# Postmix of a talking-heads attention: one 64x112 product per block of keys instead of two of 64x56

## The chip, the cores and the metric

The kernel runs on one core of one Trainium2 chip. The metric is the device time of one execution in microseconds (us). Engines: PE is TensorE (PEld are its weight loads), DVE is VectorE, ACT is ScalarE, POOL is GpSimd, SP is the engine that issues most of the DMAs.

## The reference

All in fp32. Four batches, 12 heads, 448 positions, head size 64; the result of the attention goes through an elementwise mixture (`moe`) and a soft routing over 32 slots (`moe2`), which the change doesn't touch.

```python
scores = scale * np.matmul(q, k.transpose(0, 1, 3, 2))
scores = np.einsum('bhij,hg->bgij', scores, w_pre)      # premix
scores = scores - np.max(scores, axis=-1, keepdims=True)
attn = np.exp(scores)
attn = attn / (np.sum(attn, axis=-1, keepdims=True) + 1e-09)
attn = np.einsum('bhij,hg->bgij', attn, w_post)         # postmix
out = np.matmul(attn, v)
...
h = x @ w_in; g = h - np.tanh(h); x = g @ w_out         # moe
```

## The kernel before

The program has two halves. In the first, `talking_heads` computes the attention; in the second, `moe_and_slots` does the rest. The attention works in 16 chunks of up to 120 query positions of one batch, and in slots of up to 10 positions by 12 heads of a chunk. Slots are taken in pairs, 92 of them; a pair is s and s + 1 in the main loop, and each slot has two halves x of up to 5 positions, 60 rows of (head, position).

The path of a pair, in the order in which it is issued:

- `scores` (L279): q times k for a pair of heads, in fp32r, weights of 64 rows by up to 120 columns, copied by ACT (S, L287).
- `regroup` (L304): a DMA from SP brings the rows of one slot from S into a buffer D, so that heads lie on partitions. It is issued four slots ahead (`D_AHEAD`); there are six such buffers.
- `premix` (L313): w_pre times D into the PSUM tile pm, four products of 64 by 64 pieces, then the row maximum on DVE (mx, L317).
- `expo` (L325): the exponential on ACT into e, 64 rows of one slot above 64 rows of the other, 448 keys along the free axis. `guard`, `recip` and `norm` (L331, L335, L342) make wk, the postmix weights divided by the row sums.
- `postmix` (L356), four slots after the premix (`T_LAG`): for each half x, each of four blocks c of 112 keys and each slot i, e is the stationary operand and wk (60 columns) the moving one. The result has keys on partitions and goes into the PSUM tiles tm, one per slot. Before, a block of 112 keys is taken as two halves z of 56, which land on partitions 0 to 55 and 64 to 119.
- `gather` (L370, L373, L374): ACT copies tm into aT.
- `values` (L395): aT times v, contracted over the partitions that hold keys, accumulated over the four blocks, copied by DVE into xs (L405).

Key 4p + r of a head lies at column 112 r + p, so v must lie the same way over partitions: `load_v` (L170) brings it in two transfers, one for each half of the partitions. The eight partitions 56 to 63 and the eight from 120 on hold no key; they are zeroed once in v and tm by memsets.

The order on PE is the order of the code: in an even slot the premix of the new pair, then the postmix of the pair four slots back, then score products and other jobs (`k_pair` kx, `q_half` qx, `values` vx), which a small planner places by slot with fixed costs. Beside it runs the conversion of the weights of the second half on ACT, DVE and POOL (tiles f, fa), with its loads and stores on SP.

Of the kernel before, what the change touches and what calls it, by code (L numbers as in the profile page):

```python
# [17 lines left out]
NP = NH // 2  # L18
NR = 4
JP = SEQ // NR  # L20
JH = JP // 2
IH = 5
PASS = (512, 512, 512, 256)
LATE = 12
# [108 lines left out]
def talking_heads(tc, ident, q, k, v, w_pre, w_post, xd, box, follow):  # L133
    nc = tc.nc
# [20 lines left out]
    nat_k, nat_v, nat_q = {}, {}, {}  # L155
# [3 lines left out]
    attn_t = {}  # L159
# [6 lines left out]
    def load_v(b, hf):  # L166
        t = vns[(2 * b + hf) % 3]
        src = v[b, hf * NP:(hf + 1) * NP].rearrange("h (p r) d -> p h r d", r=NR)
        for z in range(2):
            nc.sync.dma_start(out=t[64 * z:64 * z + JH], in_=src[JH * z:JH * z + JH])  # L170
        nat_v[b, hf] = t

    def load_q(n):
# [44 lines left out]
    def small_bank(shape, name, tag=None):  # L218
        if tag is None:
            tag = min("xq", key=lambda z: ready[z][turn[z]]) if box["both"] else "x"  # L220
        i = turn[tag]
        turn[tag] = 1 - i
        ready[tag][i] = 10 ** 6
        pool = ps if tag == "x" else psq

        def read():
            ready[tag][i] = now[0]

        return pool.tile(shape, FP32, tag=tag, name=name, bufs=2), read
# [65 lines left out]
    def rows(s):  # L295
        n, kk = slots[s]
        o, m = chunks[n][3][kk]
        return n, o, m
# [48 lines left out]
    def postmix(s):  # L347
        es, wks = e_t.pop(s), wk_t.pop(s)
        xs = tms
        for x in range(2):  # L350
            for c in range(NR):
                for i in range(2):
                    for z in range(2):
                        h = slice(64 * i, 64 * i + 64)
                        j = JP * c + JH * z
                        nc.tensor.matmul(  # L356
                            xs[i][64 * z:64 * z + JH, x, c], lhsT=es[x][h, j:j + JH], rhs=wks[x][h],
                            start=True, stop=True)
        tm_t[s] = xs

    def gather(s):
        for i, x in enumerate(tm_t.pop(s)):
            n, o, m = rows(s + i)
            if o == 0:
                attn_t[n] = lt.tile([128, NR, NH, CHUNK], FP32, tag="aT", name="aT", bufs=2)
            c0 = sum(z for q, z in chunks[n][3] if q < o)
            out = attn_t[n].rearrange("p r h i -> p (r h) i")
            x = x.rearrange("p x r h i -> p (r h) x i")
            if m == 2 * IH:
                nc.scalar.activation(  # L370
                    out=out[:, :, c0:c0 + m].rearrange("p a (x i) -> p a x i", x=2), in_=x, func=ACTF.Copy)
            else:
                nc.scalar.activation(out=out[:, :, c0:c0 + IH], in_=x[:, :, 0], func=ACTF.Copy)  # L373
                nc.scalar.activation(out=out[:, :, c0 + IH:c0 + m], in_=x[:, :, 1, :m - IH], func=ACTF.Copy)  # L374
# [3 lines left out]
    def keep(n, dst, src):  # L378
        if n >= NC - 2:
            (nc.sync if n == NC - 2 else nc.scalar).dma_start(out=dst, in_=src)  # L380
        else:
            plan("load", now[0] + 1, lambda: nc.sync.dma_start(out=dst, in_=src))

    def values(n, g):
        b, i0, ni, _ = chunks[n]
        a = attn_t[n]
        if g == 0:
            xs_t[n] = lt.tile([128, NP, CHUNK], FP32, tag="xs", name="xs", bufs=1)
        xs = xs_t[n]
        x, read = small_bank([128, 2, CHUNK], "vx")  # L390
        for i in range(2):
            for c in range(NR):
                for e in range(2):
                    h = 4 * g + 2 * i + e
                    nc.tensor.matmul(  # L395
                        x[64 * e:64 * e + 64, i, :ni], lhsT=nat_v[b, h // NP][:, h % NP, c, :], rhs=a[:, c, h, :ni],
                        start=(c == 0), stop=(c == NR - 1))

        def rest():
            ms = [m for _, m in chunks[n][3]]  # L400
            w, top, c = len(ms), max(ms), 0
            natural = xs[:, 2 * g:2 * g + 2, :w * top].rearrange("p a (t w) -> p a w t", w=w)
            for m in sorted(set(ms), reverse=True):
                o, z = ms.index(m), ms.count(m)
                nc.vector.tensor_copy(  # L405
                    out=natural[:, :, o:o + z, :m],
                    in_=x[:, :, c:c + z * m].rearrange("p a (w t) -> p a w t", w=z))
                c += z * m
            read()
            if g == 2:  # L410
                t0, t1, p0 = b * SEQ + i0, b * SEQ + i0 + ni, 0
                for p, size in enumerate(PASS):
                    lo, hi = max(t0, p0), min(t1, p0 + size)
                    if lo < hi:
                        keep(n, xd[p][:, :, lo - p0:hi - p0], xs[:, :, lo - t0:hi - t0])
                    p0 += size

        return rest

    start = [sum(len(c[3]) for c in chunks[:n]) for n in range(NC + 1)]  # L420
# [11 lines left out]
    def calm(kind, lo, hi):  # L432
        return min(range(lo, hi + 1), key=lambda s: (load[kind][s], s))
# [20 lines left out]
    for m in range(1, NC):  # L454
        if chunks[m][1] + CHUNK >= SEQ and m + 1 < NC:
# [3 lines left out]
            for p in range(NP):  # L459
                t = w0 + HEAD_LAG + p // 2 * w // 3 + 1 + p % 2  # L460
# [9 lines left out]
    for m in range(NC):  # L470
        step = len(chunks[m + 1][3]) // 3 if m + 1 < NC - 1 else 2
        for g in range(3 if m + 1 < NC else 0):
            lo = start[m + 1] + T_LAG + 1 + g * step
            job(calm("pe", lo, lo + step - 1) if m + 2 < NC else lo, values, m, g, dve=0.41, pe=2.0)
    for b in range(NB):
        s0 = start[b * NC // NB]
        if b:
            fetch(s0 - 12, s0 + 8, 2.7, load_v, b, 0)
        fetch(s0 + (T_LAG + 10 if b else 8), s0 + 15, 2.7, load_v, b, 1)
# [18 lines left out]
    t = 2  # L498
    for i, j in enumerate(pieces):
        due = dues[i]  # L500
        t0 = max(t, due)
        a = calm("act", t0, t0 + 1)
        x = calm("dve", a + 1, a + 1 + (a <= due))
        load["dve"][x] += 0.54
        h = calm("dve", x, x + 1)
        load["dve"][h] += 0.47
        e = calm("dve", h, h + 1)
        load["dve"][e] += 0.74
        load["act"][a] += 0.41
        t = h  # L510
# [19 lines left out]
    vns = [lt.tile([128, NP, NR, HD], FP32, tag=f"vn{i}", name="vn", bufs=1) for i in range(3)]  # L530
# [1 line left out]
    wpost = kron("wpost", post_rows, 1.0, False)  # L532
    warm = ps.tile([128, 128], FP32, tag="p", name="warm")
    tms = [ps.tile([128, 2, NR, NH, IH], FP32, tag=f"t{i}", name="tm", bufs=1) for i in range(2)]
    for z in range(2):
        nc.vector.memset(vns[0][64 * z + 32:64 * z + 64], 0.0)
    for t in tms:
        nc.vector.memset(t, 0.0)

    for p in range(3, NP):  # L540
        load_k(0, p)
    for t in ds:
        nc.gpsimd.memset(t[:4], 0.0)
    for t in vns[1:]:
        for z in range(2):
            nc.gpsimd.memset(t[64 * z + 32:64 * z + 64], 0.0)
    for _ in range(WARM):
        nc.tensor.matmul(warm, lhsT=ident, rhs=ident, start=True, stop=True)
    for p in range(NP):
        k_pair(0, p)()  # L550
        if p == 0:
            q_half(0, 0)()
        if p == 3:
            load_q(1)
            load_v(0, 0)
        if p >= 2:
            for f in scores(0, p - 2, True):
                f()
        if p == 3:
            q_half(0, 1)()  # L560
# [18 lines left out]
    while s < NS:  # L579
# [6 lines left out]
        if s % 2 == 0:  # L586
            premix(s)
            for f in late:
                f()
            late = []  # L590
            if s >= T_LAG:
                postmix(s - T_LAG)
            expo(s)
            guard(s)
        else:
            recip(s - 1)
            norm(s - 1)
            for f in late:
                f()
            late = []  # L600
            if s > T_LAG:
                gather(s - 1 - T_LAG)
# [23 lines left out]
    for u in range(NS - T_LAG, NS, 2):  # L626
        postmix(u)
        for f in late:
            f()
        late = []  # L630
        next(more)
        gather(u)
        next(more)
    for g in range(3):
        values(NC - 1, g)()
# [840 lines left out]
def fused_kernel(  # L1476
# [57 lines left out]
    with tc.manual_schedule():  # L1534
        talking_heads(
            tc, ident, q, k, v, w_pre, w_post, xd, box,
            lambda: moe_and_slots(tc, ident, xd, wi, wo, wo4, wis, (tshift, tlimit, moe2_phi, sel, sela, seld), moe2_w1, moe2_w2, out, box))
# [29 lines left out]
```

## Time and profile before

| what | value |
|---|---|
| median of 3 runs | 891.73 us |
| lowest and highest of them | 885.24, 895.21 us |
| the profiled execution | 886.23 us |
| its span, first to last instruction | 884.5 us |
| PE busy in the span | 807.9 us (91%) |
| ACT, DVE, POOL busy | 570.5, 556.7, 247.7 us |

The profile is of one execution. PE's busy time is the union of its matmuls, whose ends are modelled, so the distance between starts says more than a duration. The attention lasts until about 440 us.

### The profile page before, as it was taken

The numbers are of one execution on the slowest core, as the hardware profiler recorded it, in microseconds if no ns is written. First come the engines' busy times: TensorE is split into PE (matmuls) and PEld (weight loads), VectorE is DVE, ScalarE is ACT, GpSimd is POOL, SyncE is SP. The second block draws the span as 40 slices with busy tenths as digits, with TensorE's granted clock in tenths as the row PEclk, the third lists the DMA queues.
The fourth block names the chain that finished last, engine by engine and source line by source line (L and its number), as shares of the span: only waits on it lengthen the run. The fifth ranks groups of instructions, "written<-read, shape, count | busy, mean of one in ns | idle before, by whom it ended". The sixth has DMA issues, their size and how long they took to land.

```text
span 884.5 us, 28648 instructions
## 1 busy us (share of the span) xinstructions
PE 807.9 (91%) x11790; PEld 570.8 (65%) x11790; DVE 556.7 (63%) x1181; ACT 570.5 (64%) x1345; POOL 247.7 (28%) x428
## 2 busy tenths in 40 slices
PE   8889988799987999899899999999999999999965
PEld 6556665566665667566676667667776786964322
DVE  5357766577666777788456986566765777830104
ACT  4777887687776878798666776546664666821103
POOL 5234344334334444454303452000000003700000
PEclk9999999899999999999999999999999999999988
DMA  9787888768888788785759976678764457899998
GB/s 182 191 234 220 213 236 248 218 190 211 231 253 226 219 206 239 236 254 177 256 176 363 374 260 223 207 316 317 302 215 175 149 179 256 313 359 413 424 392 303
DMA packets 131766, 224.53 MB, mean 254 GB/s; under 512 B 44852, under 2 KB 112436, under 8 KB 128052
## 3 DMA queue, kind: packets, MB, share of 16 engines
q1 hardware_dynamic: 128288, 209.84, 74.8%
q10 hardware_dynamic: 3348, 12.87, 3.7%
q8 instruction: 93, 1.52, 0.7%
q14 instruction: 37, 0.30, 0.1%
HBM read 147.96 MB, written 36.18 MB: 208 GB/s over the span
## 4 chain that ended last, share of the span: by engine, by line
PE 50%; DMA 18%; ACT 13%; DVE 12%; issue 5%; SPq 1%; POOL 1%; ACTq 0%; POOLq 0%; DVEq 0%
PE hp L840 21%; DMA D<-S 7%; DMA ex<-in_moe_w_dram 7%; ACT e L325 6%; PE pm L313 5%; PE sc L279 5%; DVE mx L317 4%; PE vx L395 3%; PE tm L356 3%; PE gt L911 2%; ACT S L287 2%; PE kx L236 2%; PE lgp L995 2%; PE sp L1077 1%; ACT aT L370 1%
## 5 line engine op out<-in xcount | busy, mean ns | idle before, releaser
L325 ACT ACTIVATE e<-pm,mx 128x448 f32<-128x448 f32 x184 | 115.1, 631 | 86.3 <-DVE mx L317 84.9
L840 PE MATMUL hp<-xa,rg 128*128 128x512 f32 x576 | 152.7, 405 | 0.2 <-POOL rg L788 0.2
L317 DVE TENSOR_REDUCE mx<-pm 128x1 f32<-128x448 f32 x184 | 106.1, 618 | 73.5 <-PE pm L313 73.4
L356 PEld LDWEIGHTS tm<-wk,e 64*56 64x56 f32 x5888 | 104.7, 128 | 62.8 <-issue 32.4
L356 PE MATMUL tm<-wk,e 64*56 64x60 f32 x5888 | 113.5, 216 | 13.3 <-issue 7.9
L313 PE MATMUL pm<-D,wpre 64*64 64x448 f32 (+2 forms) x736 | 107.6, 565 | 18.4 <-DMA D<-S 15.2
L840 PEld LDWEIGHTS hp<-xa,rg 128*128 128x128 f32 x576 | 102.3, 188 | 28.9 <-issue 10.5
L287 ACT ACTIVATE S<-sc 120x448 f32<-120x448 f32 (+1 forms) x186 | 91.4, 553 | 4.6 <-PE sc L279 3.0
L279 PE MATMUL sc<-khi,qT 64*120 64x448 f32 (+1 forms) x384 | 83.6, 392 | 9.3 <-DVE xs L405 6.2
L342 POOL TENSOR_SCALAR wk<-wpost,rv 128x60 f32<-128x60 f32 x184 | 86.9, 503 | 16.5 <-DVE rv L335 13.8
L331 POOL TENSOR_SCALAR rv<-ss 128x2 f32<-128x2 f32 x92 | 24.5, 266 | 225.3 <-ACT e L325 194.6
L395 PE MATMUL vx<-aT,vn 128*64 128x120 f32 (+1 forms) x1536 | 83.9, 262 | 2.0 <-ACT S L287 1.3
L797 POOL TENSOR_TENSOR rg<-rg 128x384 fp32r<-128x384 f32 x24 | 23.9, 1012 | 208.8 <-DVE rg L794 205.0
L395 PEld LDWEIGHTS vx<-aT,vn 128*64 128x64 f32 x1536 | 74.7, 137 | 7.2 <-issue 3.0
L860 ACT ACTIVATE sq<-hp 128x512 f32<-128x512 f32 (+1 forms) x62 | 32.9, 530 | 68.0 <-PE hp L840 68.0
L370 ACT ACTIVATE aT<-tm 128x480 f32<-128x480 f32 x144 | 75.8, 593 | 0.1
L871 DVE SCALAR_TENSOR_TENSOR qd<-qd,sq 128x512 f32<-128x512 f32 (+1 forms) x61 | 37.6, 616 | 59.1 <-ACT mk L867 53.7
L840 PE MATMUL hp<-xb,rg 128*128 128x512 f32 x288 | 74.7, 404 | 0.0
L840 PEld LDWEIGHTS hp<-xb,rg 128*128 128x128 f32 x288 | 52.1, 188 | 16.6 <-issue 6.3
L279 PEld LDWEIGHTS sc<-khi,qT 64*120 64x120 f32 (+1 forms) x384 | 45.3, 173 | 26.1 <-PE tm L356 9.4
L71 POOL TENSOR_TENSOR fa<-fa,f 128x384 f32<-128x384 f32 x56 | 57.7, 1030 | 6.4 <-DVE f L66 2.1
L313 PEld LDWEIGHTS pm<-D,wpre 64*64 64x64 f32 (+2 forms) x736 | 23.9, 132 | 51.4 <-DMA D<-S 23.2
(199 smaller groups left out, 1391.3 us busy)
## 6 DMA issues: line engine op xcount, KB each, us to landing
ex<-in_moe_w_dram SPq DMA_DIRECT2D x21, 1536.0 KB
D<-S SPq DMA_DIRECT2D x144, 210.0 KB
rg<-wis SPq DMA_DIRECT2D x36, 768.0 KB
f<-in_moe_w_in_dram SPq DMA_DIRECT2D x32, 384.0 KB
wis<-rg ACTq DMA_DIRECT2D x16, 768.0 KB
f<-in_moe_w_out_dram SPq DMA_DIRECT2D x24, 384.0 KB
rg<-wi SPq DMA_DIRECT2D x19, 384.0 KB
wi<-fa SPq DMA_DIRECT2D x32, 192.0 KB
```

The lines of the kernel that those rows point to most:

```text
L71: eng.tensor_tensor(out=out, in0=bits(a), in1=bits(p), op=ALU.add)
L279: nc.tensor.matmul(xs[e][0][:ni], lhsT=qT[n][s, l, p, :ni], rhs=kt[s], start=(i == 0), stop=(i == 2))
L287: nc.scalar.activation(out=dst, in_=xs[e][0][:ni], func=ACTF.Copy)
L313: nc.tensor.matmul(xs[x][64 * i:64 * i + 64], lhsT=wpre[k0:k1], rhs=d[i][k0:k1], start=True, stop=True)
L317: nc.vector.tensor_reduce(out=mx[:, x:x + 1], in_=xs[x], op=ALU.max, axis=AX.X, negate=True)
L325: nc.scalar.activation(out=es[x], in_=xs[x], func=ACTF.Exp, bias=mx[:, x:x + 1], accum_out=ss[:, x:x + 1])
L342: nc.gpsimd.tensor_scalar(out=wk, in0=wpost, scalar1=rv[:, x:x + 1], scalar2=None, op0=ALU.mult)
L356: nc.tensor.matmul(xs[i][64 * z:64 * z + JH, x, c], lhsT=es[x][h, j:j + JH], rhs=wks[x][h], start=True, stop=True)
L370: nc.scalar.activation(out=out[:, :, c0:c0 + m].rearrange("p a (x i) -> p a x i", x=2), in_=x, func=ACTF.Copy)
L395: nc.tensor.matmul(x[64 * e:64 * e + 64, i, :ni], lhsT=nat_v[b, h // NP][:, h % NP, c, :], rhs=a[:, c, h, :ni], start=(c == 0), stop=(c == ...
L840: nc.tensor.matmul(hp, lhsT=r32(w[:, m, hl, cs]), rhs=r32(x_of(b, c, l)), start=(c == 0 and i == 0), stop=(c == KD - 1 and i == 2))
L871: nc.vector.scalar_tensor_tensor(out=qd, in0=qd, scalar=TG_E, in1=sq, op0=ALU.add, op1=ALU.mult)
```

## The change

The postmix takes all 112 keys of a block as the stationary operand of one product: 64 rows by 112 columns, result on partitions 0 to 111. The loop over z is gone, v comes in one transfer onto 112 partitions, the gather and the value products read 112 partitions, and the memsets of the unused partitions go.

```diff
-JH = JP // 2
...
     def load_v(b, hf):
         t = vns[(2 * b + hf) % 3]
         src = v[b, hf * NP:(hf + 1) * NP].rearrange("h (p r) d -> p h r d", r=NR)
-        for z in range(2):
-            nc.sync.dma_start(out=t[64 * z:64 * z + JH], in_=src[JH * z:JH * z + JH])
+        nc.sync.dma_start(out=t[:JP], in_=src)
...
         for x in range(2):
             for c in range(NR):
                 for i in range(2):
-                    for z in range(2):
-                        h = slice(64 * i, 64 * i + 64)
-                        j = JP * c + JH * z
-                        nc.tensor.matmul(
-                            xs[i][64 * z:64 * z + JH, x, c], lhsT=es[x][h, j:j + JH], rhs=wks[x][h],
-                            start=True, stop=True)
+                    h = slice(64 * i, 64 * i + 64)
+                    nc.tensor.matmul(
+                        xs[i][:JP, x, c], lhsT=es[x][h, JP * c:JP * c + JP], rhs=wks[x][h], start=True, stop=True)
...
-            out = attn_t[n].rearrange("p r h i -> p (r h) i")
-            x = x.rearrange("p x r h i -> p (r h) x i")
+            out = attn_t[n][:JP].rearrange("p r h i -> p (r h) i")
+            x = x[:JP].rearrange("p x r h i -> p (r h) x i")
...
-                        x[64 * e:64 * e + 64, i, :ni], lhsT=nat_v[b, h // NP][:, h % NP, c, :], rhs=a[:, c, h, :ni],
+                        x[64 * e:64 * e + 64, i, :ni], lhsT=nat_v[b, h // NP][:JP, h % NP, c, :], rhs=a[:JP, c, h, :ni],
...
-    for z in range(2):
-        nc.vector.memset(vns[0][64 * z + 32:64 * z + 64], 0.0)
-    for t in tms:
-        nc.vector.memset(t, 0.0)
...
-    for t in vns[1:]:
-        for z in range(2):
-            nc.gpsimd.memset(t[64 * z + 32:64 * z + 64], 0.0)
```

On PE, in the middle of the attention, the program before stands as follows (pm is the premix, tm the postmix, qx a turned block of q, vx a value product, sc the scores; a count here is of products, and the trace shows two matmuls for each in full fp32).

```order
L313 MATMUL pm<-D,wpre 64x448 x4
L356 MATMUL tm<-wk,e 56x60 x32
L258 MATMUL qx<-ident,qn 128x88 x3
L395 MATMUL vx<-aT,vn 64x120 x16
L313 MATMUL pm<-D,wpre 64x448 x4
L356 MATMUL tm<-wk,e 56x60 x32
L279 MATMUL sc<-khi,qT 88x448 x2
```

The same place on PE in the changed program:

```order
L311 MATMUL pm<-D,wpre 64x448 x4
L352 MATMUL tm<-wk,e 112x60 x16
L256 MATMUL qx<-ident,qn 128x88 x3
L390 MATMUL vx<-aT,vn 64x120 x16
L311 MATMUL pm<-D,wpre 64x448 x4
L352 MATMUL tm<-wk,e 112x60 x16
L277 MATMUL sc<-khi,qT 88x448 x2
```

Nothing moved: each row of 32 postmix products has become a row of 16 in the same place, and the rows around it are the same. Of the 92 postmix rows, 90 stand directly behind a premix, 43 directly before scores, and 3 directly before the next premix, in both programs.

## Rows read from the trace of the kernel before

**Rows 1.** The page's parts 1 (busy, share, instructions) and 4 (chain by engine)

```profile
PE 807.9 (91%) x11790; PEld 570.8 (65%) x11790; DVE 556.7 (63%) x1181; ACT 570.5 (64%) x1345; POOL 247.7 (28%) x428
...
PE 50%; DMA 18%; ACT 13%; DVE 12%; issue 5%; SPq 1%; POOL 1%; ACTq 0%; POOLq 0%; DVEq 0%
```

**Rows 2.** Windows: length, busy us (instructions) of each engine, PE clock, DMA share, GB/s

```profile
20.00:440.00 420.00, 376.30 (x8903) 268.82 (x8902) 283.05 (x657) 328.66 (x867) 169.74 (x343) 0.99 0.80 223
440.00:884.50 444.50, 414.03 (x2723) 288.26 (x2723) 261.02 (x502) 232.42 (x461) 65.59 (x59) 0.99 0.78 286
```

**Rows 3.** Waits of PE, 30 to 445 us: total us, times, longest us

```profile
PE pm L313 <- DMA D<-S: 14.4, 9, 3.9
PE tm L356 <- issue: 7.9, 7, 2.5
PE sc L279 <- DVE xs L405: 6.2, 14, 0.6
PE kx L236 <- ACT S L287: 2.9, 6, 0.9
PE pm L313 <- ACT e L325: 2.5, 4, 0.8
...
PE tm L356 <- ACT aT L370: 2.2, 5, 0.8
```

**Rows 4.** Weight loads by form: count, busy us, mean ns, idle us before

```profile
L356 PEld LDWEIGHTS tm<-wk,e 64*56 64x56 f32 x5888 | 104.7, 128 | 62.8 <-issue 32.4 <-POOL fa L71 10.8 <-POOL wk L342 8.2
...
L279 PEld LDWEIGHTS sc<-khi,qT 64*120 64x120 f32 x288 | 34.7, 181 | 17.4 <-PE tm L356 6.7 <-issue 2.7 <-PE sc L279 1.8
```

**Rows 5.** Timeline of PE, 202 to 207.6 us: start us, duration us, instructions

```profile
203.00 1.81 PE L395 MATMUL vx<-aT,vn 128*64 128x120 f32 x32
204.74 0.98 PE L313 MATMUL pm<-D,wpre 64*64 64x448 f32 x8
205.54 1.03 PE L356 MATMUL tm<-wk,e 64*56 64x60 f32 x64
206.51 0.47 PE L279 MATMUL sc<-khi,qT 64*120 64x448 f32 x2
206.81 0.37 PE L279 MATMUL sc<-klo,qT 64*120 64x448 f32 x2
207.02 0.37 PE L279 MATMUL sc<-khi,qT 64*120 64x448 f32 x2
```

**Rows 6.** Timeline of weight loads, 794 to 797 us: 128 columns, 32 moved

```profile
794.79 1.41 PEld L1311 LDWEIGHTS sip<-seld,tq 128*128 128x128 f32 x12
```

**Rows 7.** Timeline of PE, 775 to 777.2 us: 128 weight columns, 128 moved

```profile
775.61 1.05 PE L1258 MATMUL warm<-ident 128*128 128x128 f32 x8
```

**Rows 8.** Timeline of all engines, 108 to 115 us

```profile
110.26 0.43 PE L279 MATMUL sc<-khi,qT 64*120 64x448 f32 x1 [0.60 <-DVE xs L405]
...
114.28 0.43 PE L356 MATMUL tm<-wk,e 64*56 64x60 f32 x14 [0.94 <-issue]
```

**Rows 9.** The page's part 3: queue, packets, MB, share

```profile
q8 instruction: 93, 1.52, 0.7%
```

**Rows 10.** Timeline of all engines, first 30 us

```profile
1.35 1.34 DVE L536 MEMSET vn<- 32x1536 f32 x1 [0.37 <-issue]
...
5.99 1.06 PE L236 MATMUL kx<-ident,kn 112*64 112x112 f32 x16
...
14.51 5.63 POOL L546 MEMSET vn<- 32x1536 f32 x4
...
26.29 0.23 POOL L331 TENSOR_SCALAR rv<-ss 128x2 f32<-128x2 f32 x1 [6.15 <-ACT e L325]
```

**Rows 11.** The line that issues the loads of v: ns min/median/max

```profile
L170 SPq DMA_DIRECT2D vn<-in_v_dram x16: 448/506/1246, 8.8 to 375.3; - x16
```

**Rows 12.** The page's part 5: the gather

```profile
L370 ACT ACTIVATE aT<-tm 128x480 f32<-128x480 f32 x144 | 75.8, 593 | 0.1
```

**Rows 13.** Timeline of weight loads, 574.5 to 576 us: transposes

```profile
574.92 0.32 PEld L1065 LDWEIGHTS etp<-ident,et 32*128 32x128 f32 x4 [0.37 <-issue]
```

## The prediction

> **What bounds the kernel now.** I read the page's totals first, then the two halves of the span, then who TensorE (PE) waits for in the half that the change touches, then single products there. TensorE is busy 91% of the span and the chain of waits lies on it for half of its length [rows 1]. The postmix runs only in the attention half; the second half holds nothing that the diff touches. Between 20 and 440 us PE is busy 376.3 of 420 us, ACT 328.7, DVE 283.1, at a granted clock of 0.99, which is the 2.4 GHz level [rows 2]. So PE has 43.7 us of idle time there and nobody else is near its load: the time of this half is PE's work plus what PE waits for. The waits, from 30 to 445 us, come to 41 us in all, the largest of them for the regrouped scores D [rows 3].
>
> **The product itself.** A product of one pair of slots is 64 matmuls in the trace before (each fp32 product runs as two), and 92 pairs make the 5,888 of the profile [rows 4]. They go out in fours: two halves of the rows (i) times two halves of the keys (z), on four 64x64 pieces of the array. The row of 64 takes 1.03 us with 0.21 us for the last one [rows 5]: (1.03 - 0.21) / 63 = 13.0 ns from start to start, 52 ns for a four, 16 fours. Sixty columns are moved in these 52 ns, and 56 weight columns are loaded beneath them.
>
> After the change there are 32 matmuls in 16 steps of two. Each moves the same 60 columns, so the moving side gains nothing: the four ran side by side already. But each loads 112 weight columns instead of 56. No row of the trace shows 64 rows by 112 columns with so few moving columns, so the step is bounded by the nearest rows. Twelve loads of 128 columns with only 32 moved columns each take 1.41 us, 0.19 for the last: 111 ns per load, or 0.87 ns a column [rows 6]. A run of 8 with 128 weight columns and 128 moved columns keeps (1.05 - 0.28) / 7 = 110 ns [rows 7]: the moving lies beneath the load, and with 32 moved columns it is the load that sets the pace. On 64 rows a load grows from 128 to 181 ns between 56 and 120 columns, 0.83 ns a column [rows 4]. And where a score product starts with nothing loaded, its first pair takes 0.30 us to the next and the second 0.21 [rows 5]: 0.09 us is the bare load of 120 columns, for both row halves at once. Ends: 84 ns (0.09 x 112 / 120) and 111 ns (as for 128). I take 0.87 x 112 = 98 ns, from the row in which loads follow each other without a pause, since that is what will happen here. From the first step to the last there are 15 intervals: 15 x (98 - 52) = 0.69 us a product, x 92 = **63.5 us** more.
>
> **The change of shape.** Before, premix and postmix both use 64x64 pieces, and the first postmix weights are loaded while the premix still runs. After, the postmix uses 64 rows by the full width, as the score products do. What a change of shape costs is read at two places [rows 5]. The last two of vx start at 203.00 + 1.81 - 0.27 = 204.54 and pm at 204.74, 0.20 us later instead of the 0.10 of two vx: 0.10 late. The last four of tm start at 205.54 + 15 x 0.052 = 206.32 and sc at 206.51, 0.19 later instead of 0.05: 0.14 late, and sc then pays 0.09 for bare weights. I take 0.12. By the order of PE, 90 products follow the premix directly: +0.12 x 90 = 10.8. Forty-three are followed by scores, whose shape they now share: they lose 0.12 + 0.09 and gain 0.05, because the last step is then a full 98 ns: -0.16 x 43 = -6.9. Three are followed by the premix: +0.5. Sum **+4.4**. If changes cost nothing the term is about -2; if they cost 0.2 it is about +8.
>
> **Given back.** PE becomes 68 us heavier, and part of that lies in time in which it waits now [rows 3].
> - D: the load of slot s + 4 refills the buffer that the premix of slot s - 2 read last, so three products lie between its release and its use: 3 x 0.74 = 2.2 us more time per load. Nine waits hold 14.4 us, mean 1.6, longest 3.9. I take 11.
> - Scores behind the value copy: in the row at 110.26 [rows 8] PE stands 0.60 us for DVE's xs, and a product lies between that copy's source and the waiting score. No such wait is over 0.6: all 6.2 go.
> - kx behind ACT, and the premix behind the exponential of the pair before: 2.9 and 2.5, all under 0.9 and with a product inside: 4.5.
> - tm behind "issue", 7.9: PE stops within a product while nothing in the profile holds it (row at 114.28 [rows 8], the last 14 of 64). A queue of their own brings the instructions [rows 9]; of PE's 23,580 (11,790 matmuls and as many loads [rows 1]) 5,888 go. That it is the fetch is a guess; I take 5.
> - tm behind the gather, 2.2: stays, for the time between two products does not grow.
> Together **26.5** of 41. What is late next is again PE: ACT's 328.7 and DVE's 283.1 us fit into 460.
>
> **Edits at nothing.** The two DVE memsets of v (1.34 us each) and those of tm end before the first k product at 5.99, which waits for its load; the four on POOL (5.63 us) end at 20.14, and POOL is next wanted at 26.29 [rows 10]. Without that cover they would be worth at most 3.7 us. The eight saved issues of v (0.51 us each on SP [rows 11]) free 4 us of a queue that PE waits for only through D; bytes are the same, so I put it at 0, between -1 and +1. The gather (593 ns [rows 12]) reads the same 480 elements on fewer partitions: 0. The value products contract over 112 rows instead of 128 and move the same columns: 0.
>
> **Sum.** 63.5 + 4.4 - 26.5 = 41.4. The profiled execution took 886.23 us, 1.7 us outside its span; the median of the runs is 5.5 above it, with 885.24 to 895.21 as their spread. 886.2 + 41.4 = 927.6; I say **928**, and leave the 5.5 to the range.
>
> **Rivals.**
> - *The count of instructions sets the pace, not the load.* Then 32 of them take 32 x 13.0 = 0.42 us instead of 0.83: -38, +4, no more give-back: about 852, **faster**. For it: a mean of 13.0 ns is all that the row of 64 shows, and that could be an issue rate. Against: the loads of 128 columns at 111 ns are far from any such pace, and the 60 moved columns did not get shorter. The Trainium skill ("TensorE: Matmul & The Clock Gate", section "Wait — 56ns, not 53.3ns?") has such a floor per matmul, start to start never below about 25 ns; this trace disagrees with the figure, at 13.0 ns on four pieces.
> - *The load runs at the pace of the transposes.* Four transposes' loads of 128 columns take 0.32 us, 0.14 for the last: 60 ns each [rows 13], which for 112 columns is 53: no change per step, +4 for shapes, a few us back: 884 to 892, **not slower**. This is the case of the other side, and it decides at the point where a 112-column load fits under the 52 ns of the moving. Against: scores are no transposes and load 120 columns bare in 90 ns.
> - *The load is not hidden at all.* If a load could not run beneath a matmul on the same rows, the step would be 98 + 52 = 150 ns: 15 x 98 x 92 = 135 more, 139 less 35 back: about 990. The trace speaks against it: 110 ns for 128 columns loaded and 128 moved. The Trainium skill (same page, section "The mechanism") says that loads overlap running matmuls only where the row group differs; the 16 steps on the same two row groups would decide it.
> - *The change doesn't do what it says:* the order shows 16 products of 112x60 in place of 32 of 56x60, in the same places, so this has no chance of its own.
>
> **Chances and range.** Forecast 0.86; instruction pace 0.04; transposes' pace 0.06; nothing hidden 0.04. Within the forecast a step of 91 ns with all 41 us given back is 54 + 4 - 41 = +17, 903; 111 ns with only D's 11 given back is 81 + 4 - 11 = +74, 960. The range 902 to 958 holds nearly all of the forecast but its corners, some 8 in 10. A 1% difference is about what the spread of the three runs (1.1%) can tell from none. Faster 0.05, same 0.06, slower 0.89.
>
> **What would show it.** Right: 32 matmuls per product, starts 49 ns apart on average; a product of about 1.7 us instead of 1.03; loads of 64x112 near 174 ns; 0.1 us between premix and postmix; waits for D and xs mostly gone; the second half unchanged at 444 us. Wrong: steps near 52 ns (then the load is not the pace) or 150 (then it is not hidden); waits for D that stay or grow; a granted clock below 0.99 in the first half.

## The result and the profile after

The changed kernel takes 893.86 us (median of 20 executions, 886.41 to 900.65) where the kernel before takes 886.80 (20 executions, 883.61 to 895.21): a ratio of 1.0056, 95% interval 1.0036 to 1.0077. It is slower, as forecast, but by 0.6% and not by the 4.6% of the prediction, and so by less than the 1% that the prediction could tell from none; 893.86 lies below the range of 902 to 958. Some executions are slow ones, and the ratios compare fast executions alone, so that a ratio can differ by some 2 us from the difference of the two medians. The profiled execution has a span of 891.7 us at a granted clock of 0.991; before it was 884.5.

The page of the kernel after: part 1 (busy, share, instructions), part 3 (queues), part 4 (chain by engine) and three groups of part 5.

```profile
PE 852.7 (96%) x8846; PEld 615.0 (69%) x8846; DVE 553.5 (62%) x1177; ACT 571.6 (64%) x1345; POOL 242.8 (27%) x424
...
q8 instruction: 70, 1.15, 0.5%
...
PE 75%; DMA 11%; DVE 6%; ACT 3%; issue 3%; SPq 1%; POOL 0%; ACTq 0%; POOLq 0%; DVEq 0%
...
L352 PEld LDWEIGHTS tm<-wk,e 64*112 64x112 f32 x2944 | 152.7, 175 | 66.5 <-POOL wk L340 35.5
...
L352 PE MATMUL tm<-wk,e 64*112 64x60 f32 x2944 | 165.3, 261 | 1.6 <-ACT aT L365 1.6
...
L311 PE MATMUL pm<-D,wpre 64*64 64x448 f32 (+1 forms) x736 | 99.3, 566 | 6.0 <-DMA D<-S 5.3
```

PE's busy time grew from 807.9 to 852.7 us, its share from 91 to 96%, and the chain lies on it for three quarters of its length where it was half [rows 1]. Span less busy time is PE's idle time: 76.6 us before, 39.0 after. So PE worked 44.8 us more and stood 37.6 us less, and the difference, 7.2 us, is the difference of the spans.

Windows of the kernel after, in the columns of [rows 2]:

```profile
20.00:440.00 420.00, 412.37 (x5895) 306.60 (x5895) 280.21 (x651) 326.72 (x858) 168.41 (x338) 1.00 0.78 218
440.00:891.70 451.70, 422.77 (x2792) 294.83 (x2788) 264.16 (x508) 235.44 (x470) 67.32 (x64) 0.99 0.78 286
```

PE's idle time in the first window fell from 43.7 to 7.6 us. In the second it is 28.9 us, against 30.5 in [rows 2]. The attention ends later than the "about 440 us" of the part on the kernel before: its last value product starts at 451.9 us before and at 457.5 after. From there to the end it is 432.6 and 434.2 us, so the second half gave and took next to nothing. What PE still waits for between 30 and 445 us, in the columns of [rows 3], is this in full:

```profile
PE pm L311 <- DMA D<-S: 5.0, 4, 2.0
PE tm L352 <- ACT aT L365: 1.6, 2, 0.8
```

The product itself came out as worked out. The timeline of PE after, 206 to 210.5 us, at a place like that of [rows 5] (start, duration, instructions):

```profile
206.45 0.98 PE L311 MATMUL pm<-D,wpre 64*64 64x448 f32 x8
207.37 1.78 PE L352 MATMUL tm<-wk,e 64*112 64x60 f32 x32
208.96 0.45 PE L277 MATMUL sc<-khi,qT 64*120 64x448 f32 x2
```

A product takes 1.78 us, undisturbed, where it took 1.03 [rows 5]; the mean of all, 165.3 / 92 = 1.80, is hardly longer. With 0.26 us for its last matmul that is (1.78 - 0.26) / 31 = 49 ns from start to start, 98 ns for a step of two. The load is 175 ns (174 was forecast).

Where something else than scores follows the product, the rows stand so, in the timeline of PE before (78 to 81 us) and then after (69 to 73 us):

```profile
78.45 0.98 PE L313 MATMUL pm<-D,wpre 64*64 64x448 f32 x8
79.25 1.03 PE L356 MATMUL tm<-wk,e 64*56 64x60 f32 x64
80.21 0.99 PE L236 MATMUL kx<-ident,kn 112*64 112x112 f32 x16
```

```profile
69.15 0.98 PE L311 MATMUL pm<-D,wpre 64*64 64x448 f32 x8
70.06 1.78 PE L352 MATMUL tm<-wk,e 64*112 64x60 f32 x32
71.78 0.99 PE L234 MATMUL kx<-ident,kn 112*64 112x112 f32 x16
```

**The same group before.** Two groups of part 5 of the page before, which the prediction did not look at in this way (a group's busy time is the first number behind the first bar):

```profile
L356 PE MATMUL tm<-wk,e 64*56 64x60 f32 x5888 | 113.5, 216 | 13.3 <-issue 7.9
L313 PE MATMUL pm<-D,wpre 64*64 64x448 f32 (+2 forms) x736 | 107.6, 565 | 18.4 <-DMA D<-S 15.2
```

Divided by 92 the first is 1.23 us, 0.20 longer than the undisturbed product: 18.7 us of the busy time of before were products being held up, not products. The premix has 1.17 us a pair before and 1.08 after, where an undisturbed one takes 0.98 in both timelines. The whole balance, from these rows: bare price 92 x (1.78 - 1.03) = 69.0 us; of the busy rows of the products 69.0 - (165.3 - 113.5) = 17.2 were given back; of the premix 8.3; of the idle time 37.6; all other groups together took 44.8 - 51.8 + 8.3 = 1.3 more. 69.0 - 17.2 - 8.3 - 37.6 + 1.3 = 7.2. So 63 us were given back where the prediction took 26.5.

**One such hold-up.** Timeline of all engines before, 101.5 to 103.6 us:

```profile
101.61 1.07 ACT L370 ACTIVATE aT<-tm 128x480 f32<-128x480 f32 x2
...
102.34 0.21 PEld L356 LDWEIGHTS tm<-wk,e 64*56 64x56 f32 x4 [0.61 <-POOL fa L71]
102.37 1.42 PE L356 MATMUL tm<-wk,e 64*56 64x60 f32 x64
...
102.74 0.92 PEld L356 LDWEIGHTS tm<-wk,e 64*56 64x56 f32 x60 [0.19 <-ACT aT L370]
```

The product takes 1.42 us. Its first four matmuls run, and the fifth weight load waits for ACT's gather of an earlier product, which ends at 101.61 + 1.07 = 102.68; the load starts at 102.74. PE's own row shows no wait, because the four still run out their time (some 0.2 us each): nearly all of the 0.39 us by which the product is longer counts as busy. The wait stands in the queue of loads. Waits of PE's weight loads before, 30 to 445 us (total, times, longest):

```profile
PEld pm L313 <- DMA D<-S: 23.2, 12, 4.7
...
PEld tm L356 <- ACT aT L370: 3.7, 20, 0.2
...
PEld tm L356 <- ACT aT L374: 1.5, 8, 0.2
```

and after, where products have no such row left and D's is about a third:

```profile
PEld pm L311 <- DMA D<-S: 8.6, 5, 2.7
```

Taken product by product from the trace, the 28 products of before that hold such a wait are busy 9.9 us longer in all than 1.03 us each. The 57 whose loads wait only behind "issue", for nothing that the profile shows, hold 7.4 of the 18.7 us, and the other seven 1.4.

### The profile page after: what moved, and what is told of

It reads as the page before. It is cut to its first block, busy times and chain, and to the rows that moved or that the text cites. A ratio compares the mean times of both kernels' runs of the same rounds, so it can differ in the third digit from the quotient of the medians.

```text
span 891.7 us, 22741 instructions
## 1 busy us (share of the span) xinstructions
PE 852.7 (96%) x8846; PEld 615.0 (69%) x8846; DVE 553.5 (62%) x1177; ACT 571.6 (64%) x1345; POOL 242.8 (27%) x424
## 3 DMA queue, kind: packets, MB, share of 16 engines
q8 instruction: 70, 1.15, 0.5%
## 4 chain that ended last, share of the span: by engine, by line
PE 75%; DMA 11%; DVE 6%; ACT 3%; issue 3%; SPq 1%; POOL 0%; ACTq 0%; POOLq 0%; DVEq 0%
PE hp L828 21%; PE tm L352 15%; PE pm L311 9%; PE vx L390 8%; PE sc L277 7%; DMA ex<-in_moe_w_dram 6%; DMA D<-S 3%; PE kx L234 2%; PE gt L899 2%; PE lgp L983 2%; PE sp L1065 1%; PE qx L256 1%; DMA rg<-wi 1%; PE h L1322 1%; PE wt L952 1%
## 5 line engine op out<-in xcount | busy, mean ns | idle before, releaser
L352 PEld LDWEIGHTS tm<-wk,e 64*112 64x112 f32 x2944 | 152.7, 175 | 66.5 <-POOL wk L340 35.5
L352 PE MATMUL tm<-wk,e 64*112 64x60 f32 x2944 | 165.3, 261 | 1.6 <-ACT aT L365 1.6
L315 DVE TENSOR_REDUCE mx<-pm 128x1 f32<-128x448 f32 x184 | 106.2, 619 | 74.5 <-PE pm L311 74.5
L311 PE MATMUL pm<-D,wpre 64*64 64x448 f32 (+1 forms) x736 | 99.3, 566 | 6.0 <-DMA D<-S 5.3
L390 PE MATMUL vx<-aT,vn 112*64 112x120 f32 (+1 forms) x1536 | 83.3, 262 | 0.0
L277 PE MATMUL sc<-khi,qT 64*120 64x448 f32 (+1 forms) x384 | 78.1, 385 | 0.8 <-DVE qT L260 0.8
L390 PEld LDWEIGHTS vx<-aT,vn 112*64 112x64 f32 x1536 | 74.2, 137 | 5.0 <-issue 2.0
L365 ACT ACTIVATE aT<-tm 112x480 f32<-112x480 f32 x144 | 75.8, 592 | 0.2
L859 DVE SCALAR_TENSOR_TENSOR qd<-qd,sq 128x512 f32<-128x512 f32 (+1 forms) x61 | 37.6, 616 | 59.4 <-ACT mk L855 53.8
L277 PEld LDWEIGHTS sc<-khi,qT 64*120 64x120 f32 (+1 forms) x384 | 47.4, 173 | 8.9 <-DVE qT L260 1.3
L277 PE MATMUL sc<-klo,qT 64*120 64x448 f32 (+1 forms) x192 | 46.9, 375 | 0.0
```

What stands on the lines that cost most here:

```text
L277: nc.tensor.matmul(xs[e][0][:ni], lhsT=qT[n][s, l, p, :ni], rhs=kt[s], start=(i == 0), stop=(i == 2))
L311: nc.tensor.matmul(xs[x][64 * i:64 * i + 64], lhsT=wpre[k0:k1], rhs=d[i][k0:k1], start=True, stop=True)
L315: nc.vector.tensor_reduce(out=mx[:, x:x + 1], in_=xs[x], op=ALU.max, axis=AX.X, negate=True)
L352: nc.tensor.matmul(xs[i][:JP, x, c], lhsT=es[x][h, JP * c:JP * c + JP], rhs=wks[x][h], start=True, stop=True)
L365: nc.scalar.activation(out=out[:, :, c0:c0 + m].rearrange("p a (x i) -> p a x i", x=2), in_=x, func=ACTF.Copy)
L390: nc.tensor.matmul(x[64 * e:64 * e + 64, i, :ni], lhsT=nat_v[b, h // NP][:JP, h % NP, c, :], rhs=a[:JP, c, h, :ni], start=(c == 0), stop=( ...
```

## The experiments

In every one the kernel before ran on the same chip; "before" is its median there. What e1 to e4 gain or cost in us is worked out from the ratios, the rest from the medians.

**Is PE the bound of the first half?** Four kernels make PE lighter or heavier there.

```diff
 e1 (before):   -  for z in range(2):            +  for z in range(1):
 e2 (before):   -  for c in range(NR):           +  for c in range(NR // 2):
 e3 (before):   +  w = min(2, NR - c)
                -  xs[i][64 * z:64 * z + JH, x, c], ... rhs=wks[x][h]
                +  xs[i][64 * z:64 * z + JH, x, c:c + w], ...
                +  rhs=wks[x][h].unsqueeze(1).to_broadcast([64, w, NH, IH])
 e4 (after):    -  for c in range(NR):           +  for c in range(NR // 2):
```

> The kernel before with the second half z of every key block left out: 32 matmuls per product instead of 64, still 16 steps of 52 ns, so PE's time is the same and 5,888 of PE's 23,580 instructions go, as in the change. Slack theory (PE had about 70 us of room in the first half, 44 as waits in the profile and about 26 that it does not show as gaps; the other engines' chains held the time): 884 to 888 us, no change. Fetch theory (the 60 us that came back did so because PE has fewer instructions): 845 to 870. The prediction's own view (PE is the bound, 5 us of issue waits go): about 882.

Measured: 880.74 us, before 888.62, ratio 0.9931 (0.9902 to 0.9960): 6 us for half of the matmuls and loads.

> The kernel before with two of the four key blocks of the postmix left out: 8 steps of 52 ns instead of 16, PE lighter by 0.42 us a product, 38 us in all. Slack theory: 882 to 888, nothing to be won, since PE is not what the first half waits for. Fetch theory and the prediction's view: PE's 38 us come off, 845 to 860.

Measured: 878.22, ratio 0.9898 (0.9870 to 0.9926).

> The kernel before with 120 moved columns instead of 60 in three of four key blocks (wk read twice; the second copy is overwritten by the next block, the output is the same): 12 of 16 steps take 103 ns instead of 52, PE heavier by 0.61 us a product, 56 us in all, with the instruction count, the weight loads and the 64x64 shape of before. Slack theory: 56 us fit into the room of 70, so 887 to 893. Fetch theory: no instruction goes, so 56 less the 26 of waits that were forecast to come back: 912 to 925.

Measured: 893.01, ratio 1.0067 (1.0036 to 1.0098).

> The changed kernel with two of the four key blocks of the postmix left out (tm zeroed once at the start): 8 steps of 98 ns instead of 16, PE lighter by 0.79 us a product, 72 us in all. Slack theory: the time goes back to that of the kernel before and not below, 884 to 889. Prediction's view and fetch theory: PE was the bound on both sides, so most of the 72 comes off, 830 to 860.

Measured: 884.76, ratio 0.9964 (0.9929 to 0.9999).

Taking work from PE gains 9 us in e2 and, against the kernel after, 8 in e4, and 49 us of added work costs 6 in e3 (its tm group is busy 162.7 us, that of before 113.5). PE's work was not what set the time of the first half in the kernel before: most of what PE is spared, it waits or runs slower. The window and the waits of e2:

```profile
20.00:440.00 420.00, 361.34 (x6054) 244.44 (x6054) 285.44 (x662) 332.38 (x879) 169.43 (x343) 0.96 0.81 225
```

```profile
PE sc L279 <- DVE xs L405: 11.3, 17, 1.0
PE sc L279 <- DVE klo L245: 5.5, 9, 0.7
PE kx L236 <- ACT S L287: 5.2, 6, 1.3
```

The waits behind DVE and ACT have grown, and the granted clock of the stretch fell to 0.96. In e4 it is 0.95, in e1 and e3 1.00. A lighter PE also gets a slower clock here, at the same two levels: the mean of a stretch falls when part of it is granted 1.2 GHz. Over all executions of the whole program the mean is 0.977 in e2 against 0.982 before, and 0.974 in e4 against 0.989 after. So the clock took back a part of what e2 and e4 spared PE: the premix, which they leave alone, is busy 118.5 us in e2 (107.6 before) and 110.0 in e4 (99.3 after), though some of that can be waiting. This doubt doesn't touch e3, which adds work.

In e1 PE's undisturbed product is as long as before (16 steps of 52 ns), and yet 6 us go, with all waits behind "issue" (7.9 us in [rows 3], none in e1). So the number of PE's instructions seems to have a price of its own. The change takes 5,888 of them away; e3 keeps them all, and still has 7 us of issue waits.

**The postmix done twice**, to see the price of a product where it can't hide:

```diff
-        for x in range(2):
-            for c in range(NR):
+        for x, c in [(x, c) for x in range(2) for c in range(NR)] * 2:
```

> The changed kernel with every postmix product computed twice (the same result written again): 32 steps of 98 ns, PE heavier by 1.57 us a product, 145 us in all. Slack theory: the room was used up by the change, so from here PE's work counts in full: 893 + 145 less a few = 1025 to 1040. Rival (something other than PE sets the first half even in the changed kernel, with room left): clearly less than 120 us more, under 1010.

> The kernel before with every postmix product computed twice (same result written again): PE heavier by 0.84 us a product, 77 us in all, about what the change added (74 by the trace after), but with 5,888 matmuls and loads more instead of 2,944 fewer. If only PE's time counts, it lands where the change did, at 892 to 898. If the number of PE's instructions costs by itself (waits named issue: 7.9 us before, none after and none with half the matmuls), the waits named issue grow and the time is 905 to 925.

Measured: e6 1016.88 us, ratio 1.1427 (1.1372 to 1.1482), which is 123 us over the kernel after. It falls between the two expectations: 92 products of 16 steps of 98 ns are 144 us of new work, and some of it still hid: the premix group is busy 92.4 us in place of 99.3, the two score groups 69.3 and 37.6 in place of 78.1 and 46.9, and PE's idle time is 34.2 us in place of 39.0. In e6 PE is busy for 418.5 of the 420 us between 20 and 440. e5 took 1001.52, ratio 1.1243 (1.1161 to 1.1325): 112 us for 77 us of matmuls (92 x 16 x 52 ns), above both expectations. Waits of PE in e5, 30 to 440 us:

```profile
PE tm L356 <- issue: 44.8, 36, 3.2
PE sc L279 <- issue: 13.8, 8, 4.0
PE vx L395 <- issue: 5.8, 5, 2.9
PE kx L236 <- issue: 3.9, 3, 2.0
```

There is nothing else of size: 68 us behind "issue", no wait for D. (The attention of e5 lasts until 569 us; over all of it these four are 53.3, 17.6, 11.6 and 3.9, 86 us.) With 11,776 more instructions in the postmix the queue of instructions carries more (part 3 of the page of e5):

```profile
q8 instruction: 139, 2.28, 1.0%
```

against 93 packets before [rows 9] and 70 after. That the waits called issue are the supply of instructions fits these counts (e1 and after none, before 7.9, e5 68), but it is an inference: no row names q8 as the releaser. Nor does the count alone set them: e6 has as many instructions on PE and as many packets (93) as the kernel before, and no such wait; there the same number is spread over a longer time.

**What makes D late, and what else?** e7 and e8 take the conversion's arithmetic off ACT and DVE in the kernel before and after (a copy on POOL remains), e9 gives D eight buffers for six, e10 and e11 take the conversion's 56 loads away together with its arithmetic (its stores remain, of a constant tile).

```diff
 e7, e8:    -  f64_abs(...); f64_shift(...); f64_head(...); f64_tail(...); f64_sum(...)
            +  self.nc.gpsimd.tensor_copy(out=bits(a), in_=bits(p))
 e9:        -  DB = 6                                 +  DB = 8
 e10, e11:  -  self.nc.sync.dma_start(out=r..., in_=src[:, a0:a0 + self.KD // 2])
            +  self.t[j] = self.still
```

> The kernel before without the arithmetic of the weight conversion in the first half (one ACT and five DVE operations a piece left out, POOL copies one word instead; loads and stores stay; the second half gets other weights). It takes some 33 us from ACT and over 100 from DVE between 20 and 440 us. If the room of PE comes from the other engines' queues (scores, maxima and copies standing behind conversion pieces), the first half gets shorter and the time falls to 855 to 875. If it comes from the D loads and their queue on SP, which stay, 880 to 887.

> The changed kernel with the same left out. Slack theory: PE holds the first half here whatever ACT and DVE do, so 885 to 892, nearly as with the conversion; beside the kernel before without conversion arithmetic the change then costs 15 to 35 us instead of 5, if that one got faster. Rival (both kernels are held by the same chain): both fall by the same amount and the 5 us stay.

Measured: 888.24 (before 889.70; ratio 0.9960, 0.9927 to 0.9994) and 893.14 (1.0048, 1.0009 to 1.0088). Taking 41% of DVE's work of the first half (283.1 us to 167.4 in the same window) changes neither kernel by more than a few us. ACT's and DVE's arithmetic of the conversion by itself is not what holds PE.

> The kernel before with eight D buffers instead of six: a D load waits for a premix two slots further back, and what stands behind it on SP's queue goes earlier too. If the D loads and SP's queue hold the first half of the kernel before, the 14 us of PE's waits for D go and the time falls by 8 to 20 us, to 868 to 880. If other chains hold it, 883 to 888.

Measured: 890.12, ratio 1.0019 (0.9983 to 1.0055): nothing. Waits of PE in e9, 30 to 440 us:

```profile
PE vx L395 <- issue: 7.8, 4, 3.9
PE tm L356 <- issue: 7.4, 9, 2.3
...
PE pm L313 <- DMA D<-S: 5.0, 5, 2.3
PE sc L279 <- issue: 3.9, 2, 2.7
```

The wait for D fell from 14.4 us to 5.0, and PE waits behind "issue" instead, 19.1 us in these rows where it was 8.6 (7.9 in [rows 3] and 0.7 before vx); the granted clock of the window is 0.97, but this is one execution, and the mean over the twelve, 0.983, is that of before, 0.982. Nine us of waiting went and the time stayed: something else took its place, by this trace the waits behind "issue".

> The kernel before with the weight conversion of the first half reduced to its stores (a constant tile is stored; 56 loads of 384 KB and all arithmetic left out): 21.5 MB fewer through the DMA engines, which are busy 0.80 between 20 and 440 us. If the DMA load is what holds the first half (D loads landing late, instructions arriving late), the waits for D and those named issue go and the time falls to 850 to 872. If not, 880 to 888, as without the arithmetic.

> The changed kernel with the same left out. PE holds its first half with or without these loads: 884 to 892. If the kernel before gets faster by them, the change then costs 15 to 35 us instead of 5, which is the price of the load-bound step laid bare; if neither moves, the room of PE has another source.

Measured: e10 857.47, before 889.67, ratio 0.9643 (0.9603 to 0.9683); e11 882.70, ratio 0.9933 (0.9909 to 0.9957). The kernel before gains 32 us when these loads go, the kernel after only 11 from its 893.86. The change costs 25 us in place of 7. Window of e10, and then of e11:

```profile
20.00:440.00 420.00, 394.83 (x9169) 285.74 (x9170) 183.91 (x408) 321.17 (x845) 103.61 (x289) 0.99 0.63 186
```

```profile
20.00:440.00 420.00, 416.99 (x6013) 312.63 (x6012) 169.55 (x380) 306.08 (x815) 99.45 (x286) 1.00 0.57 172
```

The DMA share falls from 0.80 to 0.63 and D is hardly ever late (0.7 us in the second group below). The loads' bytes, their place in SP's queue and the arithmetic went together here; e7 clears the arithmetic alone, and no run tells the other two apart. Groups of PE by line in e10:

```profile
L338 PE MATMUL tm<-wk,e 64*56 64x60 f32 x5888 | 109.8, 215 | 11.6 <-issue 5.1 <-ACT aT L352 3.5 <-POOL wk L324 0.5
L295 PE MATMUL pm<-D,wpre 64*64 64x448 f32 (+1 forms) x736 | 97.2, 561 | 4.0 <-ACT e L307 2.6 <-DMA D<-S 0.7 <-POOL wk L324 0.6
```

The premix's 107.6 us became 97.2 (1.06 a pair), so most of the hold-ups in it, 10.4 of 17.4 us, went with the loads. The product's 113.5 became 109.8 only (1.19 a pair, 15 us over 92 undisturbed ones), and 25.2 us of idle time remain in the window: the part of the cover that has nothing to do with these loads.

**What is that part?** e13 puts e1's edit on e10, e14 that of e3.

> The kernel before without the conversion's loads (857.5 us), and with one half of the keys only in the postmix: half of its matmuls and weight loads are left out, in the same 16 steps, so that a product takes the same time undisturbed. If the number of instructions is what still stretches the products there (the 5,888 matmuls of the postmix are busy 109.8 us where 92 undisturbed products of 1.03 are 95), the issue waits go and the time falls by 10 to 20 us, to 838 to 848. If ACT and DVE hold the rest, it stays within 4 us, 853 to 859.

> The kernel before without the conversion's loads (857.5 us), with 120 moved columns in three of four blocks (part of the output is overwritten by the next block): about 56 us more of TensorE's time at the same number of instructions. With the loads in place this cost 6 us. If the loads' traffic alone was the cover, now 40 to 56 us, 897 to 913. If waits on ACT, DVE and instructions cover part of it as they do for the change (25 of 69 left to pay), about 20 to 30 us, 877 to 888.

Measured: e13 852.34, before 888.90, ratio 0.9579 (0.9538 to 0.9620); e14 873.93, ratio 0.9821 (0.9784 to 0.9857). Groups and waits of e13:

```profile
L338 PE MATMUL tm<-wk,e 64*56 64x60 f32 x2944 | 106.2, 216 | 9.6 <-ACT aT L352 5.0 <-POOL wk L324 0.5 <-ACT aT L356 0.3
```

```profile
PE tm L338 <- ACT aT L352: 5.0, 11, 0.8
PE pm L295 <- ACT e L307: 2.6, 4, 0.8
...
PEld tm L338 <- ACT aT L352: 5.3, 24, 0.2
```

e13 lies 5 us under e10, just outside either expectation. The issue waits went, as in e1 and for about as much, but the products stayed long: 106.2 us, 1.15 a pair, with half of the matmuls left out. So the number of instructions is worth some 5 to 6 us with and without the loads (the intervals of e10 and e13 overlap, so the second figure is weak), and it is not what stretches the products. The gather on ACT is, by the trace of e13: 34 products, 24 and 10 by the two lines of the gather, hold a load that waits for it, and these hold 11.1 of the 12.7 us by which the 92 exceed an undisturbed one of e13 (1.016 us). e14 adds 47 us of product time (its tm group is busy 157.2 us, that of e10 109.8) and costs 16, less than the 20 to 30 expected and far from the 40 to 56 that would hold if the loads alone were the cover.

**The edits at nothing.** e12 puts v back into two transfers, of 56 partitions each, in the kernel after, and keeps memsets of v and tm on DVE.

```diff
-        nc.sync.dma_start(out=t[:JP], in_=src)
+        for z in range(2):
+            nc.sync.dma_start(out=t[JP // 2 * z:JP // 2 * z + JP // 2], in_=src[...])
```

> The changed kernel with v brought in two transfers of 56 partitions and the memsets of v and tm kept on DVE at the start. The prediction put these edits at nothing, so the time is that of the changed kernel, 891 to 896. If one transfer or the missing memsets won something that hid part of the price, 897 to 905.

Measured: 896.09, ratio 1.0100 (1.0060 to 1.0140). The median lies between the two expectations, and the interval overlaps that of the change itself, 1.0036 to 1.0077, so what these edits bring is not told apart from zero; at the middle of both it would be 4 us gained. The gather took 593 ns before and 592 after, as said.

## Why the prediction was wrong

Its mechanism for the product held and its direction held; one term, what is given back, was mis-sized, and by itself puts the time out of range.

- **The product itself: right.** Forecast 98 ns a step and 174 ns a load; measured 98 and 175. The rivals fall with it: the pace of instructions (52 ns or less a step), the pace of the transposes (53 ns) and the load that isn't hidden (150 ns). On the last, the Trainium skill ("TensorE: Matmul & The Clock Gate", section "The mechanism") lets loads overlap matmuls only where the row group differs; this trace disagrees, with steps of 98 ns on the same two row groups where load and move one after the other would take 150.
- **The change of shape: too small.** From premix to product it is 0.91 to 0.92 us after against 0.80 [rows 5], close to the 0.12 taken. But from the start of the product to what follows it, scores come 1.59 us later in place of 0.97, and kx 1.72 in place of 0.96. From premix to scores that is 0.74 us more, from premix to the others 0.87; for 43 and 49 products 74 us in all, where 63.5 + 4.4 = 67.9 was forecast. So the shapes cost about 10 us, above the 8 that the prediction gave for 0.2 us a change. Against these 74 us, counted from start to start, 67 came back; against the 69.0 of the rows' lengths it is the 63 of the balance.
- **Given back: this is the step that failed.** It was 26.5 us (its four terms add up to 26.7), and the trace after shows 63: 37.6 in idle time and 25.5 in rows counted as busy. Of the waits that it listed it was near: D gave back 9.4 on PE (11 forecast), xs all 6.2, kx and e 5.4 (4.5), issue 7.9 (5). It counted nothing for small waits not listed, which went too. And it held that PE waits only where PE's rows have gaps. The products of before were 18.7 us longer than undisturbed ones, the premixes 17.4 (1.17 against 0.98), and these gave back 17.2 and 8.3. The group's busy time by its count, 113.5 / 92, set beside the 1.03 us of the one product that it did read, would have shown 18.7 us that no list of waits holds.
- **"tm behind the gather stays, for the time between two products does not grow": wrong.** In the rows of PE it was 2.2 us and is 1.6. But 28 further waits for the same gather stood in the queue of loads, in products that were 9.9 us longer by the trace, and all are gone. The gather is one step behind; a product that is 0.75 us longer gives ACT this time.
- **"The time of this half is PE's work plus what PE waits for"**, read as a sum in which work weighs fully, is what stands behind both. e2, e3 and e4 show how little PE's work weighed: -9, +6 and -8 us for tens of us of it. After the change it weighs: e6 pays 123 of 144.
- **Range.** Its lower corner took 91 ns a step and 41 us given back as the most that there was. A give-back of 63 lies outside every corner.

What gave the room is shown in part. The loads of the conversion (with its arithmetic) are the largest single supplier found: without them the price is 25 us (e10, e11) and most of the premix's hold-ups go. Half the number of PE's instructions is worth 5 to 6 us (e1, e13); that the change, which also halves them, earned this much back for itself is an inference. The waits behind ACT's gather are read from the trace, and e13 shows that they are not a matter of the instruction count; no run removed them by themselves. A further part is the clock: over all executions its mean is 0.982 before and 0.989 after. In the trace of before PE stands 3.94 us for D, until 168.66; the clock between 160 and 210 us is 0.93 (1.00 after), and the value product at 172.59 takes 2.25 us in place of the 1.81 of [rows 5]. How the 63 us split exactly between these stays open, because a wait that is removed can turn into another one (e9). Of the other kernels that compute all of the reference none is faster than the kernel before: e9 is the same, e12 is like the kernel after, e3, e5 and e6 are slower.

## What to carry to other kernels

Before pricing an edit on the busiest engine, divide each group's busy time by its count and set it beside one undisturbed instance: here the excess was mostly waiting that no list of PE's waits shows. Read the waits of the weight loads beside those of the matmuls. An engine that is busy 90% of a stretch may still have its period set by the transfers, the instructions and the engines around it, and then added work costs little until the idle time and the excess are used up (6 of 49 us in e3, 7 of the 74 of the change), and most of its price behind that (123 of 144 in e6). In the rows here in which fewer columns are moved than loaded (60 and 112, 32 and 128), the load set TensorE's step (98 and 111 ns), and merging two narrow loads that ran side by side into a wide one nearly doubled the step, from 52 to 98 ns.

## What the hardware showed that was not expected

- The number of instructions appears to be a load on PE: doubling the postmix at 64 matmuls a product brought 68 us of waits behind "issue" between 30 and 440 us for 77 us of work in all (e5); halving the postmix's instructions at equal PE time gained 6 us (e1).
- A lighter PE was granted a lower clock in the same stretch: 0.96 in e2 and 0.95 in e4, against 0.99 and 1.00 in the kernels that they were made from; and the heavier PE of the change a higher one, 0.989 against 0.982 over all executions.
- Two more buffers for a late transfer moved the wait and not the time: 14.4 us for D became 5.0, the time stayed at a ratio of 1.0019 (e9).
